# Loops on two engines, aligned loads and a reordered tail in a two-block decode attention kernel

## The chip, the cores and the metric

The kernel runs on one core of one Trainium2 chip. The metric is the device time of one execution in microseconds.

## What is computed

Two independent attention blocks, A and B, decode one token each for a batch of two, with 32 heads of width 192 and a cache of 8192 keys and values per head. Their outputs stand side by side. In block A every head has its own cache too (`rep` is 1), so both blocks do the same work.

```python
def block(x, k_cache, v_cache, wq, wo):          # A and B alike
    B, Sq, D = x.shape                           # 2, 1, 640
    Hq, Dh = 32, 192
    q = (x @ wq).reshape(B, Sq, Hq, Dh).transpose(0, 2, 1, 3)
    scores = jnp.einsum("bhqd,bhkd->bhqk", q, k_cache) * (Dh ** -0.5)
    p = jax.nn.softmax(scores, axis=-1)
    o = jnp.einsum("bhqk,bhkd->bhqd", p, v_cache)
    return o.transpose(0, 2, 1, 3).reshape(B, Sq, Hq * Dh) @ wo
out = concatenate([block(A...), block(B...)], axis=-1)
```

All inputs are bf16. The four caches hold some 805 MB, and each byte of them is used once.

## The kernel before

The work is cut into 64 **units**. A unit is two heads of one batch entry of one block: its K and its V are one load each of 6144 KB, with 64 partitions for each of the two heads and 128 positions of 192 elements (49152 bytes) on every partition. A large tensor `big` in SBUF holds three buffers of that size (`kv`, taken in turn) and two product buffers `prod`, one for a quarter of a unit. Before the loop over units, the query weights lie in `big` as well, and all queries are computed at once into `qall`; at the end the output weights are loaded into buffers that have come free.

For one unit u, in four chunks c of 32 positions:

- VectorE multiplies the chunk of K by the query, `dve_mul`, into `prod[c % 2]` (signal `m, u, c`).
- TensorE sums each position's 192 products to 16 partial sums in PSUM with 12 products by an identity matrix, `pe_sum` (signal `s, u, c`).
- VectorE reduces these 16 to one score, `dve_red` (`r, u, c`); after the last chunk it takes the maximum, `dve_max`.
- GpSimd spreads the maximum over the partitions, `pool_ar`; ScalarE negates it, `act_nb`, and takes the exponentials and their sums, `act_exp`.
- TensorE adds up the sums, `pe_l`, and multiplies the exponentials by V in 64 products, `pe_pv` (`pv, u`). This stands one slot later, after the scores of unit u + 1; for unit 61 it stands two slots later, after the scores of unit 63, next to that of unit 62.
- VectorE takes the reciprocal, and adds the halves (`dve_rc`, `dve_ohi`, `dve_osum`); ScalarE scales the row and puts it back into `qall` (`act_of`).

Each compute engine's instructions are put in a table by slot and order within the slot (`put`), sorted, and added to that engine's `_Stream`. `resolve` turns the named signals into semaphore counts and drops waits that an earlier wait already covers. `emit` writes the instructions; with a `period` it looks (`_find`) for the longest run of slots that repeats every `period` slots with steadily growing counts, writes the part before it in full, then one hardware loop whose waits compare with a register, then the rest in full. In the kernel before, TensorE alone is given `period=6`; VectorE, ScalarE and GpSimd are written out in full.

SyncE issues all large loads in one order: query weights, K 0, then K u and V u - 1 in turn, with K 63 ahead of V 61 near the end, V 62 and V 63, then the output weights in ten pieces. A load waits until its buffer is free: until the last product of the K that it replaces (`m, u, 3`) or the V product (`pv, u`). V 63 is loaded in two halves with signals of their own, both issued after `m, 63, 3`. Block A's output weights wait for `pv, 61` and `s, 63, 3` (they cover V 61's buffer and the product buffers); the first three pieces of block B's wait for `pv, 62`, and the last five for the first half of V 63's product. A matmul `pe_out` for each row of weights then makes the output.

SBUF tensors lie in the order in which they are declared, each rounded up to 32 bytes; the framework puts four small constants of 32 bytes each ahead of the kernel's first tensor. In the kernel before that first tensor is `big`.

Of the kernel before, what the change touches and what calls it, by code (L numbers as in the profile page):

```python
# [5 lines left out]
ALU = mybir.AluOpType  # L6
# [6 lines left out]
class _Stream:  # L13

    def __init__(self, name, sem, reg):
        self.name = name
        self.sem = sem
        self.reg = reg
        self.count = 0
        self.ops = []  # L20

    def add(self, fn, waits=(), sig=None, tag=None):
        if sig is not None:
            self.count += 1
            assert sig not in self.reg, sig
            self.reg[sig] = (self.sem, self.count)
        self.ops.append((fn, tuple(waits), sig is not None, tag))

    def resolve(self):
        waited = {}  # L30
# [14 lines left out]
            out.append((fn, need, has_sig, tag))  # L45
        return out

    def emit(self, eng, period=None):
        ops = self.resolve()
        if period is None:  # L50
            self._emit(eng, ops)
            return
        first, plen, reps, steps = self._find(ops, period)
        self._emit(eng, ops[:first])
        with eng.Fori(0, reps) as it:
            self._emit(eng, ops[first:first + plen], it, steps)
        self._emit(eng, ops[first + plen * reps:])

    def _find(self, ops, period):
# [44 lines left out]
def build_kernel(nc, blocks, out):  # L104
# [5 lines left out]
    TC = 32  # L110
# [21 lines left out]
    with ExitStack() as es:  # L132
        sb = lambda name, shape, dt: es.enter_context(nc.sbuf_tensor(name, shape, dt))
        ps = lambda name, shape, dt: es.enter_context(nc.psum_tensor(name, shape, dt))
        sem = lambda name: es.enter_context(nc.semaphore(name))

        big = sb("big", [128, NBUF * BUFE + 2 * PRODE], BF16)
        qall = sb("qall", [128, NU, Dh], BF16)
        pb = [sb(f"pb{i}", [128, 2 * T], BF16) for i in range(2)]
# [4 lines left out]
        mg = [sb(f"mg{i}", [128, 2], F32) for i in range(2)]  # L144
        nb = [sb(f"nb{i}", [128, 1], F32) for i in range(2)]
        rs = [sb(f"rs{i}", [128, 2], F32) for i in range(2)]
        rc = [sb(f"rc{i}", [2, 1], F32) for i in range(2)]
        ones = sb("ones", [128, 1], F32)
        ident = sb("ident", [128, 128], BF16)
        place = sb("place", [2, 256], BF16)  # L150
        o_hi = sb("o_hi", [2, Dh], F32)
        o_sum = sb("o_sum", [2, Dh], F32)
        oTz = [sb(f"oTz{k}", [128, WR, 6], BF16) for k in range(NBLK)]
        out_sb = [sb(f"out_sb{k}", [4, NH2], BF16) for k in range(NBLK)]
        actd = sb("actd", [128, 2], F32)

        ops = [ps(f"ops{i}", [128, 512], F32) for i in range(2)]
        scps = [ps(f"scps{i}", [128, TC, DG], F32) for i in range(NCH)]
# [63 lines left out]
        def key(name, *idx):  # L222
            for i in idx:
                if i < 0:
                    return None
            return (name,) + tuple(idx)
# [48 lines left out]

        def dve_mul(u, c):
            t = kv[buf["k", u]]
            q = qall[:, u, :].unsqueeze(1).broadcast_to([128, TC, Dh])
            return lambda eng: eng.tensor_tensor(prod[c % 2], t[:, c * TC:(c + 1) * TC, :], q, ALU.mult)  # L279

        def dve_red(u, c):
            return lambda eng: eng.tensor_reduce(sc[u % 2][:, c * TC:(c + 1) * TC], scps[c][:], AXL.X, ALU.add)  # L282
# [1 line left out]
        def dve_max(u):  # L284
            def fn(eng):
                for s in range(2):
                    r = slice(64 * s, 64 * s + 64)
                    ins = eng.tensor_reduce(mp[u % 2][r, s:s + 1], sc[u % 2][r, :], AXL.X, ALU.max)  # L288
                return ins
            return fn  # L290

        def dve_rc(u):
            return lambda eng: eng.reciprocal(rc[u % 2][:], ops[u % 2][0:2, QW:QW + 1])  # L293
# [5 lines left out]
            return lambda eng: eng.tensor_tensor(o_sum[:], ops[u % 2][0:2, 0:Dh], o_hi[:], ALU.add)  # L299

        def act_of(u):
            return lambda eng: eng.activation(qall[0:2, u, :], o_sum[:], ACTF.Identity, scale=rc[u % 2][:])  # L302

        def act_nb(u):
            def fn(eng):
                for s in range(2):
                    r = slice(64 * s, 64 * s + 64)
                    ins = eng.activation(nb[u % 2][r, :], mg[u % 2][r, s:s + 1], ACTF.Identity, scale=-scale)  # L308
                return ins
            return fn  # L310

        def act_exp(u):
            def fn(eng):
                for s in range(2):
                    r = slice(64 * s, 64 * s + 64)
                    dst = pb[u % 2][r, :].rearrange("p (g a j s) -> p g a j s", a=2, j=JB, s=2)[:, :, :, :, s]
                    ins = eng.activation(dst, sc[u % 2][r, :].rearrange("p (g j a) -> p g a j", j=JB, a=2),  # L317
                                         ACTF.Exp, bias=nb[u % 2][r, :], scale=scale, accum_out=rs[u % 2][r, s:s + 1])
                return ins
            return fn  # L320
# [28 lines left out]
        def pe_sum(c):  # L349
            def fn(eng):  # L350
                for j in range(NJ):
                    ins = eng.matmul(scps[c][:], ident[:], prod[c % 2][:, :, j * DG:(j + 1) * DG],  # L352
                                     start=(j == 0), stop=(j == NJ - 1))
                return ins
            return fn

        def pe_l(u):
            return lambda eng: eng.matmul(ops[u % 2][0:2, QW:QW + 1], rs[u % 2][:], ones[:], start=True, stop=True)  # L358

        def pe_pv(u, j0, j1):  # L360
            vv = kv[buf["v", u]].rearrange("p (j a) d -> p j (a d)", a=2)

            def fn(eng):
                for j in range(j0, j1):
                    j0s = 4 * JB * (j // JB) + 2 * (j % JB)
                    ins = eng.matmul(ops[u % 2][0:MP, 0:QW], pb[u % 2][:, j0s:j0s + MP], vv[:, j, :],  # L366
                                     start=(j == 0), stop=(j == TJ - 1))
                return ins
            return fn
# [27 lines left out]
        def put(eng, slot, order, fn, waits, sig, tag=None):  # L397
            t = tabs[eng].setdefault(slot, [])
            t.append((order, len(t), fn, waits, sig, tag))
# [12 lines left out]
        for u in range(NU):  # L412
            for c in range(NCH):
                w = [("k", u), ("qa", u // B), ("qx", u // B), back("s", u, c, 2)]
                if u == 0:
                    w.append(("pq", NP - 1))
                put("dve", u, 2 + 2 * c, dve_mul(u, c), w, ("m", u, c))
                put("dve", u, 2 + 2 * min(c + 1, NCH - 1) + 1, dve_red(u, c),
                    [("s", u, c), key("mx", u - 2), key("exp", u - 2)], ("r", u, c))
                put("pe", u, 0, pe_sum(c),  # L420
                    [("m", u, c), back("r", u, c, NCH), ("id1",), ("qx", NP - 1), ("qa", NP - 1)], ("s", u, c), ("s", c))
            put("dve", u, 12, dve_max(u), [("r", u, NCH - 1), key("ar", u - 2), ("init",)], ("mx", u))
            put("pool", u, 0, pool_ar(u), [("mx", u), key("nb", u - 2)], ("ar", u))
            put("act", u, 0, act_nb(u), [("ar", u), key("exp", u - 2)], ("nb", u))
            put("act", u, 1, act_exp(u), [("nb", u), key("pv", u - 2), key("l", u - 2), ("init",)], ("exp", u))
            w0 = [("exp", u), key("os", u - 2), key("rc", u - 2), ("init",)]
            pslot = u + 2 if u == LASTU - 2 else u + 1
            put("pe", pslot, 2, pe_l(u), w0, ("l", u), ("l", u % 2))
            cuts = VCUT.get(u)
            if cuts is None:  # L430
                put("pe", pslot, 3, pe_pv(u, 0, TJ), [("v", u)], ("pv", u), ("pv", u % 2, buf["v", u]))
            else:
                for c, (t0, t1) in enumerate(zip(cuts[:-1], cuts[1:])):
                    put("pe", pslot, 3 + 0.01 * c, pe_pv(u, t0 // 2, t1 // 2), [("v", u, c)],
                        ("pv", u) if t1 == T else ("pv", u, c))
            put("dve", u + 2, 20, dve_rc(u), [("pv", u), key("of", u - 2)], ("rc", u))
            put("dve", u + 2, 21, dve_ohi(u), [("pv", u), key("os", u - 1)], ("oh", u))
            put("dve", u + 2, 22, dve_osum(u), [("oh", u), key("of", u - 1)], ("os", u))
            put("act", u + 2, 4, act_of(u), [("os", u), ("rc", u)], ("of", u))

        E1, E2 = NU, NU + 1
        for hp in range(NP):
# [25 lines left out]
        for i, (kind, u) in enumerate(loads):  # L468
            w = [done(i - NBUF)]
            if i in (1, 2):  # L470
                w = [("pq", PPB * i - 1)]
            for n, fn in enumerate(ld_kv(kind, u)):
                S_sp.add(fn, waits=w if n == 0 else [])
        for n in range(len(pieces)):
            S_sp.add(ld_wo(n), waits=pieces[n][4])
        S_sp.add(out_dma(NBLK - 1, 1), waits=[("oev", NBLK - 1)])
# [25 lines left out]
        with nc.Block() as block:  # L502
            @block.sync
            def _(eng):
                S_sp.emit(eng)

            @block.gpsimd
            def _(eng):
                S_pool.emit(eng)

            @block.vector
            def _(eng):
                S_dve.emit(eng)

            @block.scalar
            def _(eng):
                S_act.emit(eng)

            @block.tensor
            def _(eng):  # L520
                S_pe.emit(eng, period=6)
# [49 lines left out]
```

## Time and profile before

| | |
|---|---|
| three runs | 1953.11 us median (1952.76 to 1954.46) |
| profiled execution | 1952.38 us |
| its span, first to last instruction | 1950.6 us, 17823 instructions |
| HBM read | 836.77 MB, 429 GB/s over the span |
| granted TensorE clock, mean | 0.943 |

The profile records one execution. A page gives busy times, the span in 40 slices, DMA queues and the chain of work that ended last; further views list instructions in order of time, windows of the span, and the sequencers' instructions by line. [...]

### The profile page before, as it was taken

To read this page: it belongs to the slowest core of one execution; us is meant where nothing else is said; L and a number is where in the kernel's file an instruction comes from. 1 tells how busy PE (TensorE), PEld (TensorE's weight loads), DVE (VectorE), ACT (ScalarE), POOL (GpSimd) and SP (SyncE) were. 2 spreads that over 40 slices of the span, in tenths; PEclk is the share of its full clock that TensorE was granted. 3 is DMA by queue.
4 is the path that set the end of the run, shared out by engine and by line. 5 is a ranking of instruction groups with operands and counts; after the bars stand their busy time and mean duration, and the time that the engine had idled before them with its cause. 6 is when DMAs were issued, how large, how long until landed. Compare 5 with 4: busy or idle time off the path is not lost.

```text
span 1950.6 us, 17823 instructions
## 1 busy us (share of the span) xinstructions
PE 1536.1 (79%) x7781; PEld 747.1 (38%) x7781; DVE 1121.0 (57%) x901; ACT 142.3 (7%) x519; POOL 28.0 (1%) x80
## 2 busy tenths in 40 slices
PE   4787877877877877877777878877888877877889
PEld 2343433433433333433333434433433433333445
DVE  3865565565565565565575565565565565565560
ACT  2100000000000000000000000000000000000000
POOL 0000000000000000000000000000000000000000
PEclk9898999999999999999998988999988999998999
DMA  9999999999999999999999999999999999999998
GB/s 415 433 423 433 433 434 434 432 430 431 433 435 433 434 431 430 433 434 434 434 433 430 432 433 433 434 435 429 433 431 435 433 434 431 432 431 433 433 413 338
DMA packets 20361, 837.20 MB, mean 429 GB/s; under 512 B 2268, under 2 KB 2280, under 8 KB 2920
## 3 DMA queue, kind: packets, MB, share of 16 engines
q1 hardware_dynamic: 20308, 836.77, 99.5%
q8 instruction: 18, 0.29, 0.1%
q14 instruction: 15, 0.12, 0.0%
q10 hardware_dynamic: 20, 0.01, 0.0%
HBM read 836.77 MB, written 0.01 MB: 429 GB/s over the span
## 4 chain that ended last, share of the span: by engine, by line
DMA 47%; PE 32%; DVE 20%; issue 0%; ACT 0%; SPq 0%
DMA big<-in_B_k_cache_dram 24%; DMA big<-in_A_k_cache_dram 21%; PE ops L366 18%; DVE big L279 18%; PE scps L352 12%; DVE sc L282 2%; DMA big<-in_B_wq_dram 2%; PE scps L344 1%; PE outps L388 1%; PE scps L388 1%; PE ops L358 0%; DVE mp L288 0%; PE oTps L375 0%; ACT out_sb L327 0%; DVE qall L269 0%
## 5 line engine op out<-in xcount | busy, mean ns | idle before, releaser
L279 DVE TENSOR_TENSOR big<-big,qall 128x6144 bf16<-128x6144 bf16 x256 | 852.9, 3352 | 512.0 <-DMA big<-in_B_k_cache_dram 258.4
L352 PE MATMUL scps<-big,ident 128*128 128x512 bf16 x3072 | 793.1, 417 | 386.2 <-DVE big L279 386.1
L366 PE MATMUL ops<-big,pb 128*34 128x384 bf16 x4096 | 676.6, 326 | 0.0
L352 PEld LDWEIGHTS scps<-big,ident 128*128 128x128 bf16 x3072 | 307.1, 105 | 864.9 <-DVE big L279 479.8
L366 PEld LDWEIGHTS ops<-big,pb 128*34 128x34 bf16 x4096 | 395.6, 98 | 258.8
L282 DVE TENSOR_REDUCE sc<-scps 128x32 f32<-128x512 f32 x256 | 176.2, 688 | 218.3 <-PE scps L352 218.3
L308 ACT ACTIVATE nb<-mg 64x1 f32<-64x1 f32 x128 | 25.7, 201 | 1703.0 <-POOL mg L260 1702.3
L317 ACT ACTIVATE pb<-sc,nb 64x128 bf16<-64x128 f32 x128 | 55.8, 436 | 11.4 <-PE ops L366 8.5
L260 POOL PARTITION_ALL_REDUCE mg<-mp x64 | 25.8, 404 | 1852.6 <-DVE mp L288 1852.6
L344 PE MATMUL scps<-big,xbc 128*128 128x384 bf16 x160 | 30.8, 361 | 14.2 <-DMA big<-in_A_wq_dram 10.9
L288 DVE TENSOR_REDUCE mp<-sc 64x1 f32<-64x128 f32 x128 | 35.9, 280 | 3.1
L269 DVE CAST qall<-scps 64x192 bf16<-64x192 f32 x64 | 22.7, 354 | 21.3 <-PE scps L344 18.6
L302 ACT ACTIVATE qall<-o_sum,rc 2x192 bf16<-2x192 f32 x64 | 29.0, 453 | 21.8 <-DVE o_sum L299 20.2
L293 DVE RECIPROCAL rc<-ops 2x1 f32<-2x1 f32 x64 | 9.9, 155 | 30.8 <-PE ops L366 28.8
L344 PEld LDWEIGHTS scps<-big,xbc 128*128 128x128 bf16 x160 | 17.0, 107 | 27.7 <-DMA big<-in_A_wq_dram 10.9
L317 ACT ACTIVATION_READ_ACCUMULATOR pb<-sc,nb 64x1 f32 x128 | 23.7, 185 | 0.0
L296 DVE COPY o_hi<-ops 2x192 f32<-2x192 f32 x64 | 22.3, 348 | 2.0
L299 DVE TENSOR_TENSOR o_sum<-ops,o_hi 2x192 f32<-2x192 f32 x64 | 22.1, 345 | 2.2
L273 ACT ACTIVATE qall<-scps 64x192 bf16<-64x192 f32 x64 | 20.8, 325 | 34.5 <-DVE qall L269 32.8
L358 PEld LDWEIGHTS ops<-ones,rs 128*2 128x2 f32 x128 | 5.5, 82 | 26.3 <-issue 26.3
L388 PE MATMUL outps<-big,oTz 128*4 128x320 bf16 x96 | 13.4, 299 | 0.0
L388 PE MATMUL scps<-big,oTz 128*4 128x320 bf16 x96 | 13.2, 299 | 0.0
(27 smaller groups left out, 49.3 us busy)
## 6 DMA issues: line engine op xcount, KB each, us to landing
big<-in_A_k_cache_dram SPq DMA_DIRECT2D x32, 6144.0 KB, 30.0
big<-in_A_v_cache_dram SPq DMA_DIRECT2D x32, 6144.0 KB, 28.1
big<-in_B_k_cache_dram SPq DMA_DIRECT2D x32, 6144.0 KB, 29.0
big<-in_B_v_cache_dram SPq DMA_DIRECT2D x31, 6144.0 KB, 27.9
big<-in_A_wq_dram SPq DMA_DIRECT2D x1, 7680.0 KB, 22.3
big<-in_B_wq_dram SPq DMA_DIRECT2D x1, 7680.0 KB, 39.9
big<-in_B_v_cache_dram SPq DMA_DIRECT2D x2, 3072.0 KB, 18.4
big<-in_A_wo_dram SPq DMA_DIRECT2D x1, 4480.0 KB, 19.3
```

What stands on the lines that cost most here:

```text
L260: return lambda eng: eng.partition_all_reduce(mg[u % 2][:], mp[u % 2][:], 128, bass.bass_isa.ReduceOp.max)
L269: return lambda eng: eng.tensor_copy(qall[ro, B * hp + 1 - s, :], qps[hp % NCH][ri, s * Dh:(s + 1) * Dh])
L279: return lambda eng: eng.tensor_tensor(prod[c % 2], t[:, c * TC:(c + 1) * TC, :], q, ALU.mult)
L282: return lambda eng: eng.tensor_reduce(sc[u % 2][:, c * TC:(c + 1) * TC], scps[c][:], AXL.X, ALU.add)
L288: ins = eng.tensor_reduce(mp[u % 2][r, s:s + 1], sc[u % 2][r, :], AXL.X, ALU.max)
L302: return lambda eng: eng.activation(qall[0:2, u, :], o_sum[:], ACTF.Identity, scale=rc[u % 2][:])
L308: ins = eng.activation(nb[u % 2][r, :], mg[u % 2][r, s:s + 1], ACTF.Identity, scale=-scale)
L317: ins = eng.activation(dst, sc[u % 2][r, :].rearrange("p (g j a) -> p g a j", j=JB, a=2), ACTF.Exp, bias=nb[u % 2][r, :], scale=scale, acc ...
L344: ins = eng.matmul(qps[hp % NCH][:, 0:QW], xbc[:, blk, c, :], wq_t[blk][:, c, off:off + QW], start=(c == 0), stop=(c == DC - 1))
L352: ins = eng.matmul(scps[c][:], ident[:], prod[c % 2][:, :, j * DG:(j + 1) * DG], start=(j == 0), stop=(j == NJ - 1))
L366: ins = eng.matmul(ops[u % 2][0:MP, 0:QW], pb[u % 2][:, j0s:j0s + MP], vv[:, j, :], start=(j == 0), stop=(j == TJ - 1))
L388: ins = eng.matmul(oacc[blk][0:4, 0:NH2], oTz[blk][:, i, 2 - 2 * half:6 - 2 * half], wo[:, i - r0, half * NH2:(half + 1) * NH2], start=(i ...
```

## The change

VectorE and ScalarE get `period=6` as TensorE has it. So that their instructions can stand in a loop, each gets a tag that repeats every six units, and those that address a row of `qall` by the unit take it from a register inside the loop (`row`). Five small tensors are declared ahead of `big`. The chunks 2 and 3 of unit 63's scores get order 4 in TensorE's slot, so that unit 61's row sum and V product (orders 2 and 2.1) stand between chunks 1 and 2; unit 62's get orders 4.5 and 4.6. The halves of V 63 wait apart: the first for `m, 63, 1`, the second for `m, 63, 3`.

```diff
@@ class _Stream
+        self.base = None
...
-        self.ops.append((fn, tuple(waits), sig is not None, tag))
+        self.ops.append((fn, tuple(waits), sig is not None, (-2, object()) if tag is None else tag))
...
+    def row(self, u):
+        return slice(u, u + 1) if self.base is None else bass.ds(self.base + u, 1)
...
         with eng.Fori(0, reps) as it:
+            self.base = it * period
             self._emit(eng, ops[first:first + plen], it, steps)
+        self.base = None
@@ build_kernel
+        actd = sb("actd", [128, 2], F32)
+        rc = [sb(f"rc{i}", [2, 1], F32) for i in range(2)]
+        o_hi = sb("o_hi", [2, Dh], F32)
+        ones = sb("ones", [128, 1], F32)
         big = sb("big", [128, NBUF * BUFE + 2 * PRODE], BF16)
...
-        rc = [sb(f"rc{i}", [2, 1], F32) for i in range(2)]
-        ones = sb("ones", [128, 1], F32)
...
-        o_hi = sb("o_hi", [2, Dh], F32)
...
-        actd = sb("actd", [128, 2], F32)
...
-            q = qall[:, u, :].unsqueeze(1).broadcast_to([128, TC, Dh])
-            return lambda eng: eng.tensor_tensor(prod[c % 2], t[:, c * TC:(c + 1) * TC, :], q, ALU.mult)
+            return lambda eng: eng.tensor_tensor(prod[c % 2], t[:, c * TC:(c + 1) * TC, :],
+                                                 qall[:, S_dve.row(u), :].broadcast_to([128, TC, Dh]), ALU.mult)
...
-            return lambda eng: eng.activation(qall[0:2, u, :], o_sum[:], ACTF.Identity, scale=rc[u % 2][:])
+            return lambda eng: eng.activation(qall[0:2, S_act.row(u), :], o_sum[:].unsqueeze(1), ACTF.Identity, scale=rc[u % 2][:])
...
-                put("dve", u, 2 + 2 * c, dve_mul(u, c), w, ("m", u, c))
+                put("dve", u, 2 + 2 * c, dve_mul(u, c), w, ("m", u, c), ("m", c, u % 6))
...
-                put("pe", u, 0, pe_sum(c),
+                put("pe", u, 4 if u == LASTU and c >= 2 else 0, pe_sum(c),
...
-            put("dve", u, 12, dve_max(u), [("r", u, NCH - 1), key("ar", u - 2), ("init",)], ("mx", u))
+            put("dve", u, 12, dve_max(u), [("r", u, NCH - 1), key("ar", u - 2), ("init",)], ("mx", u), ("mx", u % 6))
...
-            put("pe", pslot, 2, pe_l(u), w0, ("l", u), ("l", u % 2))
+            pe_o = 4.5 if u == LASTU - 1 else 2
+            put("pe", pslot, pe_o, pe_l(u), w0, ("l", u), ("l", u % 2))
...
-                put("pe", pslot, 3, pe_pv(u, 0, TJ), [("v", u)], ("pv", u), ("pv", u % 2, buf["v", u]))
+                put("pe", pslot, pe_o + 0.1, pe_pv(u, 0, TJ), [("v", u)], ("pv", u), ("pv", u % 2, buf["v", u]))
...
             for n, fn in enumerate(ld_kv(kind, u)):
-                S_sp.add(fn, waits=w if n == 0 else [])
+                if (kind, u) == ("v", LASTU):
+                    w = [("m", LASTU, VCUT[u][n + 1] // TC - 1)]
+                S_sp.add(fn, waits=w)
...
-                S_dve.emit(eng)
+                S_dve.emit(eng, period=6)
...
-                S_act.emit(eng)
+                S_act.emit(eng, period=6)
```

The other instructions of VectorE and ScalarE in a slot get tags of the same form (`dve_red`, `act_nb`, `act_exp`, `dve_rc`, `dve_ohi`, `dve_osum`, `act_of`).

More of the change, by code (lines that the diff above doesn't have):

```diff
@@ L416, in build_kernel @@
                     w.append(("pq", NP - 1))
-                put("dve", u, 2 + 2 * c, dve_mul(u, c), w, ("m", u, c))
+                put("dve", u, 2 + 2 * c, dve_mul(u, c), w, ("m", u, c), ("m", c, u % 6))
                 put("dve", u, 2 + 2 * min(c + 1, NCH - 1) + 1, dve_red(u, c),
-                    [("s", u, c), key("mx", u - 2), key("exp", u - 2)], ("r", u, c))
-                put("pe", u, 0, pe_sum(c),
+                    [("s", u, c), key("mx", u - 2), key("exp", u - 2)], ("r", u, c), ("r", c, u % 6))
+                put("pe", u, 4 if u == LASTU and c >= 2 else 0, pe_sum(c),
                     [("m", u, c), back("r", u, c, NCH), ("id1",), ("qx", NP - 1), ("qa", NP - 1)], ("s", u, c), ("s", c))
-            put("dve", u, 12, dve_max(u), [("r", u, NCH - 1), key("ar", u - 2), ("init",)], ("mx", u))
+            put("dve", u, 12, dve_max(u), [("r", u, NCH - 1), key("ar", u - 2), ("init",)], ("mx", u), ("mx", u % 6))
             put("pool", u, 0, pool_ar(u), [("mx", u), key("nb", u - 2)], ("ar", u))
-            put("act", u, 0, act_nb(u), [("ar", u), key("exp", u - 2)], ("nb", u))
-            put("act", u, 1, act_exp(u), [("nb", u), key("pv", u - 2), key("l", u - 2), ("init",)], ("exp", u))
+            put("act", u, 0, act_nb(u), [("ar", u), key("exp", u - 2)], ("nb", u), ("nb", u % 6))
+            put("act", u, 1, act_exp(u), [("nb", u), key("pv", u - 2), key("l", u - 2), ("init",)], ("exp", u), ("exp", u % 6))
             w0 = [("exp", u), key("os", u - 2), key("rc", u - 2), ("init",)]
             pslot = u + 2 if u == LASTU - 2 else u + 1
-            put("pe", pslot, 2, pe_l(u), w0, ("l", u), ("l", u % 2))
+            pe_o = 4.5 if u == LASTU - 1 else 2
+            put("pe", pslot, pe_o, pe_l(u), w0, ("l", u), ("l", u % 2))
             cuts = VCUT.get(u)
             if cuts is None:
-                put("pe", pslot, 3, pe_pv(u, 0, TJ), [("v", u)], ("pv", u), ("pv", u % 2, buf["v", u]))
+                put("pe", pslot, pe_o + 0.1, pe_pv(u, 0, TJ), [("v", u)], ("pv", u), ("pv", u % 2, buf["v", u]))
             else:
@@ L435, in build_kernel @@
                         ("pv", u) if t1 == T else ("pv", u, c))
[L436 to L439, printed above, removed]
+            put("dve", u + 2, 20, dve_rc(u), [("pv", u), key("of", u - 2)], ("rc", u), ("rc", u % 6))
+            put("dve", u + 2, 21, dve_ohi(u), [("pv", u), key("os", u - 1)], ("oh", u), ("oh", u % 6))
+            put("dve", u + 2, 22, dve_osum(u), [("oh", u), key("of", u - 1)], ("os", u), ("os", u % 6))
+            put("act", u + 2, 4, act_of(u), [("os", u), ("rc", u)], ("of", u), ("of", u % 6))
         E1, E2 = NU, NU + 1
```

## The prediction

> **What bounds the kernel now.** I read the page first: engines, slices, DMA queues, the chain's shares, the costliest group.
>
> ```profile
> PE 1536.1 (79%) x7781; PEld 747.1 (38%) x7781; DVE 1121.0 (57%) x901; ACT 142.3 (7%) x519; POOL 28.0 (1%) x80
> ...
> DMA  9999999999999999999999999999999999999998
> GB/s 415 433 423 433 433 434 434 432 430 431 433 435 433 434 431 430 433 434 434 434 433 430 432 433 433 434 435 429 433 431 435 433 434 431 432 431 433 433 413 338
> ...
> q14 instruction: 15, 0.12, 0.0%
> ...
> DMA 47%; PE 32%; DVE 20%; issue 0%; ACT 0%; SPq 0%
> ...
> L279 DVE TENSOR_TENSOR big<-big,qall 128x6144 bf16<-128x6144 bf16 x256 | 852.9, 3352 | 512.0 <-DMA big<-in_B_k_cache_dram 258.4
> ```
>
> The DMA engines are full in every slice but the last, and VectorE idles 512.0 us before its products, waiting for K: 8.0 us in each of 64 units. So only what shortens the stream of loads, or the tail behind it, can count. The chain in order of time clocks the stream, since VectorE's first product of a unit starts when its K has landed.
>
> ```profile
> 275.70 3.37 DVE big L279
> ...
> 1733.88 3.37 DVE big L279
> ...
> 1792.96 3.37 DVE big L279
> ...
> 1822.95 28.13 DMA big<-in_B_k_cache_dram
> 1851.11 6.63 DVE big L279 x2
> ...
> 1862.20 3.28 DVE big L279
> ```
>
> From 1792.96 to 1851.11 four loads of 6144 KB land, 14.54 us each (58.15 / 4). From 1733.88 to 1792.96 four more take 59.08: 0.93 longer. The DMA view of each stretch (the longer first) shows a difference:
>
> ```profile
> q8 instruction: 1, 0.02, 0.1%
> q14 instruction: 1, 0.01, 0.0%
> ```
> ```profile
> q8 instruction: 2, 0.03, 0.2%
> ```
>
> The longer one holds a fetch of instructions on q14, 8 KB each (0.12 MB in 15 packets on the page). The shorter has none, and its two fetches on q8 cost the landing nothing. Between 275.70 and 1851.11 lie 54 units, 108 loads: 1575.41 us against 108 x 14.5375 = 1570.05. The 5.36 us over are 5.8 steps of 0.93, so six.
>
> Whose fetches? VectorE's program is written out in full, and the windows view counts it over that stretch:
>
> ```profile
> 275.70:1851.10 1575.40, 1242.38 (x6157) 597.47 (x6158) 925.22 (x702) 99.94 (x378) 19.15 (x54) 0.94 1.00 433
> ```
>
> Its 702 instructions and two queued waits in each of 54 units (130 in all, a row below) make 810: 135 to each of six fetches, 61 bytes apiece in 8 KB. ScalarE's 378 would need about three. I take the six as VectorE's.
>
> A fetch occupies one DMA engine of 16; that it delays the landing each time means that this engine is the latest already, and falls further behind. The windows view of the tail shows such an engine (the last two columns are DMA share and GB/s), and the DMA view gives the time to landing of V 62, issued when unit 62's last product ends (1862.20 + 3.28 = 1865.5):
>
> ```profile
> 1884.00:1886.00 2.00, 2.00 (x10) 0.68 (x8) 2.00 (x1) 0.00 (x0) 0.00 (x0) 1.00 0.80 344
> 1886.00:1888.00 2.00, 0.90 (x6) 0.42 (x6) 1.66 (x2) 0.00 (x0) 0.00 (x0) 1.00 0.46 197
> 1940.00:1941.00 1.00, 1.00 (x9) 0.61 (x8) 0.00 (x0) 0.00 (x0) 0.00 (x0) 1.00 0.55 205
> ...
> 1942.00:1943.00 1.00, 1.00 (x9) 0.64 (x8) 0.00 (x0) 0.00 (x0) 0.00 (x0) 1.00 0.10 41
> 1943.00:1944.00 1.00, 1.00 (x9) 0.60 (x8) 0.00 (x0) 0.00 (x0) 0.00 (x0) 1.00 0.06 23
> ...
> 1945.00:1946.00 1.00, 1.00 (x9) 0.64 (x8) 0.00 (x0) 0.00 (x0) 0.00 (x0) 1.00 0.03 13
> ```
> ```profile
> big<-in_B_v_cache_dram SPq DMA_DIRECT2D x1, 6144.0 KB, 29.2
> ```
>
> At 1886 to 1888 half of the engines have nothing left (0.46), yet V 62 lands at 1894.7: most engines are some 7 us ahead of the last. At the end a share of 0.06, one engine of 16, works alone from 1943 to about 1945.5.
>
> **The change, part by part.** *Loops on VectorE and ScalarE.* VectorE's 901 instructions and 130 waits (1031) shrink to what is written out (projection and four units, about 124; the last eight units, about 110) and one body of six units. TensorE has such a loop already; its waits cost this:
>
> ```profile
> L96 PEldq ALU_OP  x279: 32/32/42, 132.9 to 1691.4; - x140
> L96 DVEq EVENT_SEMAPHORE  x130: 21/21/49, 57.3 to 1921.9; - x130
> ...
> L55 PEldq COMPARE_BRANCH  x9: 76/208/243, 301.9 to 1701.6; - x9
> ```
>
> Per unit I estimate 13 instructions, two queued waits, ten register operations for waits and twelve for the query's row (three for each of four products): 37, times six is 222. Together about 456, or 3.4 blocks of 135 where there were 7.6. The difference is 4.2, and fetches are whole: 4 or 5 fall away, 3 to 6 with the error of my count. I take 5, since the block in which the loop ends already reaches into the last units: 5 x 0.93 = 4.65 us off every landing of the last units. (ScalarE's body is shorter still; its fetches hit an engine that is not latest, and count nothing.)
>
> The loop's own cost: 22 register operations x 32 ns + 208 ns / 6 = 0.74 us a unit, hidden under VectorE's 8.0 us of waiting for K, and under the queue of loads (the load issued at 1822.95 needs 28.13 us for 14.54 of work). Without that cover it would be 54 x 0.74 = 40 us. A product whose query row is addressed by a register stands nowhere in this trace: between 0 and the 2.0 us that the cover allows each of four products. A gain has no reason here, since the tile and shape stay. I take 0; the sequencer rows, tens of ns, are the nearest.
>
> *Alignment of the loads.* Four constants of 32 bytes lie ahead of `big` in before, so its rows start 128 bytes past a multiple of 256; the change puts 896 bytes more in front (32 + 32 + 32 + 768 + 32), 1024 in all. Every load of this trace starts 128 past such a multiple, so none shows a price; the nearest row is the steady 14.54 us. I take 0, and bound it by rival B on one side and as much loss on the other.
>
> *V product of unit 61 amid unit 63's scores.* TensorE's rows (timeline, then the chain):
>
> ```profile
> 1873.90 8.31 PE L352 MATMUL scps<-big,ident 128*128 128x512 bf16 x24 [3.13 <-DVE big L279]
> 1883.25 2.76 PE L352 MATMUL scps<-big,ident 128*128 128x512 bf16 x12 [1.04 <-DVE big L279]
> 1887.11 2.76 PE L352 MATMUL scps<-big,ident 128*128 128x512 bf16 x12 [1.10 <-DVE big L279]
> ```
> ```profile
> 1889.88 0.17 PE ops L358 x4
> 1890.05 20.91 PE ops L366 x128
> ...
> 1911.34 10.51 PE ops L366 x64
> ...
> 1935.34 13.05 PE scps L388 x96
> 1948.40 0.02 issue
> 1948.42 0.43 ACT out_sb L327
> ```
>
> After the second chunk (1882.2) TensorE waits 1.04 and 1.10 us for VectorE, then never again until 1948.40: the tail is TensorE's. V 61 is there by then (below), so its 64 products (half of 20.91) and their row sums fill these gaps, and chunks 2 and 3 follow without a wait: 2.14 us off TensorE's end. VectorE's products 2 and 3 need only chunks 0 and 1, so the release of K 63 does not move. Unit 63's last chunk ends some 3.7 us later than now (1893.6, worked out below, against 1889.9), and with it its reductions, maximum and exponentials; their first user on TensorE, its V product, stands behind unit 62's 10.5 us. TensorE now waits for V 61 in the middle of the scores; the landing, 1851.1 (issued when K 62 lands) + 29.0 = 1880.1, lies 2.1 us ahead of that place, and both ends move together.
>
> ```profile
> big<-in_B_v_cache_dram SPq DMA_DIRECT2D x1, 6144.0 KB, 29.0
> ```
> ```profile
> 1900.58 0.81 SPq L234 DMA_DIRECT2D big<-in_A_wo_dram  x2
> ```
>
> The first output weights wait for V 61's product and unit 63's scores: now issued when chunk 3 ends, 1887.1 + 2.76 + 10.5 - 2.1 - 4.65 = 1893.6 in place of 1900.58. The queue is then still full of V 63.
>
> *V 63's halves apart.* The first half waits for product 1 of unit 63 instead of product 3, some 10 us earlier. Behind it on SP's queue stand only its other half and the output weights, which wait for later things. It fills the hole of 1884 to 1888, (0.20 + 0.54) x 2 = 1.5 us of the engines that are ahead. The latest engine never ran dry, so this alone moves no end, but it keeps the engines ahead from becoming the next limit.
>
> *Sum.* TensorE's end moves by 4.65 + 2.14 = 6.8. The last output weights are the other limit: the late engine finishes about 1945.5, half a microsecond to land, four products of 13.05 / 96 = 0.14 after that: 1946.6 against 1948.40, 1.8 us to spare. So the end moves by at most 4.65 + 1.8 = 6.45; I take 6.4. The profiled execution took 1952.38 (span 1950.6); it becomes 1946.0. The median of the runs, 1953.11, stands 0.73 above it: 1946.7.
>
> **Rivals.** *B, aligned loads are faster.* 128 bytes more on each row of 49152 (6144 KB over 128 partitions) would be 0.26%, 0.038 us a load, 5.1 us over 837 MB. Then 1946.7 - 5.1 = 1941.6. For it: the rate never passes 435 in the slices; against: nothing shows where the missing part goes. The Trainium skill ("DMA: Bandwidth & Descriptors", How a descriptor splits into AXI transactions) says that a transfer off a 256-byte boundary pays for the bytes below its start, which is this price; no run here shows it. Chance 0.18.
>
> *C, fewer fetches fall away,* three instead of five (a longer body than I count), or another engine takes over as latest at that depth: 2.8 + 1.8 = 4.6, 1948.5. Chance 0.14.
>
> *D, the late engine is late by nature* and the fetches only coincide; the loops then bring nothing, the late engine's weights bind, and 1.8 us are left: 1951.3. Against it: the steps. The Trainium skill ("DMA: Bandwidth & Descriptors", Latency and other measured facts) calls two of the 16 DMA engines usually slower, and puts it down to transfers issued from GpSimd; these are issued from SP. Chance 0.07.
>
> *E, slower: the loop refetches its body.* If VectorE's 222 instructions, 1.6 blocks, are fetched again in each of eight later passes, 16 fetches replace the 5: (16 - 5) x 0.93 = 10.2 us, less 1.8: 1961.5. It decides from about one fetch a pass on. Against it, TensorE's loop body of some 1360 instructions, running from 133 to 1701, shows no q8 fetch between 320 and 1720 (DMA view; q8 would stand between the two lines):
>
> ```profile
> q1 hardware_dynamic: 13865, 606.00, 100.2%
> q14 instruction: 10, 0.08, 0.0%
> ```
>
> Chance 0.07.
>
> **How the numbers follow.** Forecast 0.54 (own range 1945 to 1948), B 0.18, C 0.14, D 0.07, E 0.07. A run of this kernel can tell about 0.2%, 3.9 us. Forecast, B and most of C (0.12) are faster: 0.84; the rest of C and D: 0.09; E: 0.07. The range leaves out D, E and B's far edge: 1941.2 to 1949.6.
>
> **What would show it.** Right: q14 falls from 15 packets to under ten; the chain's VectorE piece at 1851.11 starts near 1846.5; after 276 the loads land 14.54 apart without steps; a V product of 64 stands between two blocks of 24 score matmuls and the weights are issued near 1893.6; the last score-bank matmul ends near 1942. B shows as loads 14.50 apart. Wrong: steps of 0.93 that return every pass, VectorE's wait for K falling under 1 us a unit, or a lone late engine of the same length at the end.

## The result, and the profile after

The changed kernel takes 1941.68 us (median of five runs, 1941.25 to 1942.44) against 1953.05 for the kernel before: 11.4 us less, a ratio of 0.9941 with a 95% interval of 0.9927 to 0.9956. The forecast was 1946.7. The profiled execution took 1941.25, its span 1939.5.

The page, DMA side. Its two queues of the kind "instruction" are q8 and q14. In the runs below only q14's count changes (15, 10 or 7) when VectorE's or ScalarE's program does; q8 stays at 18. As before, the engines are full in every slice but the last; the rate is a little higher, and q14 holds 7 fetches of instructions in place of 15.

```profile
DMA  9999999999999999999999999999999999999998
GB/s 416 433 430 435 434 434 430 434 437 434 431 434 437 434 433 431 438 434 433 431 438 434 433 431 438 433 434 432 437 434 433 432 437 434 433 431 436 432 429 374
...
q14 instruction: 7, 0.06, 0.0%
```

The chain in order of time, start and duration in us. A DMA piece ends when a K has landed.

```profile
1056.82 30.00 DMA big<-in_B_k_cache_dram
...
1114.80 30.01 DMA big<-in_B_k_cache_dram
...
1172.79 30.02 DMA big<-in_B_k_cache_dram
...
1752.68 30.14 DMA big<-in_B_k_cache_dram
...
1810.68 31.10 DMA big<-in_B_k_cache_dram
1841.78 0.02 issue
```

Four loads take 58.00 us (from 1114.80 + 30.01 to 1172.79 + 30.02), 14.50 each, where the kernel before took 14.54. One step is still there: from 1782.82 to 1841.78 it is 58.96. K 62 lands at 1841.78; before, it was 1851.08, 9.3 us later. Five steps of 0.96 that are gone make 4.8, and 123 loads at 0.036 less make 4.4: together 9.2, nearly all of it.

TensorE's tail in the timeline (start, duration, what; idle time and its end in brackets):

```profile
1865.73 7.57 PE L358 MATMUL scps<-big,ident 128*128 128x512 bf16 x24 [3.12 <-DVE big L284]
1873.23 0.19 PE L364 MATMUL ops<-ones,rs 128*2 128x1 f32 x2
1873.35 10.57 PE L372 MATMUL ops<-big,pb 128*34 128x384 bf16 x64
1883.86 5.35 PE L358 MATMUL scps<-big,ident 128*128 128x512 bf16 x24
1889.14 0.19 PE L364 MATMUL ops<-ones,rs 128*2 128x1 f32 x2
```

Unit 61's 64 V products stand between two blocks of 24 score products, and the waits of 1.04 and 1.10 us are gone. TensorE then works without a pause to the last row of the chain below, 1937.28, where it ended at 1948.40 before: 11.1 us, of which 9.3 came with the landings and 1.8 in the tail.

```profile
1924.23 13.05 PE scps L394 x96
1937.28 0.02 issue
```

The 1.8 is a balance of three things. The two waits bring 2.14, and the first 24 score products of unit 63 take 7.57 us in place of 8.31, 0.74 more. But these products start 23.95 us after K 62's landing (1865.73 - 1841.78), where it was 22.82 before: 1.13 lost. The first 12 score products of unit 62, behind that landing, took 2.76 us before and take 4.24 now, and VectorE waits for them. Timeline of before, then chain and window of the changed kernel (the 0.50 is the granted TensorE clock; in the window 1854 to 1858 of before it was 1.00):

```profile
1854.52 2.76 PE L352 MATMUL scps<-big,ident 128*128 128x512 bf16 x12 [0.58 <-DVE big L279]
```
```profile
1845.22 4.24 PE scps L358 x12
```
```profile
1847.00:1849.00 2.00, 2.00 (x6) 0.73 (x5) 1.43 (x1) 0.00 (x0) 0.00 (x0) 0.50 1.02 442
```

Why the granted clock was lower at that place stays open.

The windows view of the end (last two columns DMA share and GB/s) answers to the lone engine of before:

```profile
1930.00:1931.00 1.00, 1.00 (x10) 0.60 (x8) 0.00 (x0) 0.00 (x0) 0.00 (x0) 1.00 1.01 408
...
1934.00:1935.00 1.00, 1.00 (x10) 0.64 (x8) 0.00 (x0) 0.00 (x0) 0.00 (x0) 1.00 0.38 152
1935.00:1936.00 1.00, 1.00 (x9) 0.62 (x8) 0.00 (x0) 0.00 (x0) 0.00 (x0) 1.00 0.19 77
1936.00:1937.00 1.00, 1.00 (x10) 0.52 (x7) 0.00 (x0) 0.00 (x0) 0.00 (x0) 1.00 0.01 5
```

All engines are busy to 1931, and in the microsecond to 1936 the share is 0.19, three engines of 16: they end closer together.

### The profile page after: what moved, and what is told of

It is laid out like the page before. It is cut to its first block, busy times and chain, and to the rows that moved or that the text cites. A ratio compares the mean times of both kernels' runs of the same rounds, so it can differ in the third digit from the quotient of the medians.

```text
span 1939.5 us, 18491 instructions
## 1 busy us (share of the span) xinstructions
PE 1507.2 (78%) x7781; PEld 738.2 (38%) x7781; DVE 1120.2 (58%) x901; ACT 142.3 (7%) x519; POOL 28.0 (1%) x80
## 4 chain that ended last, share of the span: by engine, by line
DMA 48%; PE 28%; DVE 18%; issue 6%; DVEq 0%; ACT 0%; SPq 0%; another core or an unknown queue 0%
DMA big<-in_B_k_cache_dram 25%; DMA big<-in_A_k_cache_dram 21%; PE ops L372 18%; DVE big L284 16%; PE scps L358 7%; DVE sc L288 2%; DMA big<-in_B_wq_dram 2%; PE scps L350 1%; PE outps L394 1%; PE scps L394 1%; PE ops L364 0%; DVEq L284 0%; DVE mp L294 0%; PE oTps L381 0%; ACT out_sb L333 0%
## 5 line engine op out<-in xcount | busy, mean ns | idle before, releaser
L284 DVE TENSOR_TENSOR big<-big,qall 128x6144 bf16<-128x6144 bf16 x256 | 852.9, 3352 | 521.5 <-DMA big<-in_B_k_cache_dram 270.1
L358 PE MATMUL scps<-big,ident 128*128 128x512 bf16 x3072 | 765.1, 405 | 404.4 <-DVE big L284 404.4
L358 PEld LDWEIGHTS scps<-big,ident 128*128 128x128 bf16 x3072 | 298.8, 103 | 863.3 <-DVE big L284 503.3
L308 ACT ACTIVATE qall<-o_sum,rc 2x192 f32 (+1 forms) x64 | 29.0, 453 | 19.9 <-DVE o_sum L305 18.3
```

Of the source, the lines that this page charges most:

```text
L308: return lambda eng: eng.activation(qall[0:2, S_act.row(u), :], o_sum[:].unsqueeze(1), ACTF.Identity, scale=rc[u % 2][:])
```

## Experiments

The forecast left one question: its terms came out, but 5 us more did. Theory T is that three causes add up (five fetches fewer, aligned loads, the tail). The main rival R is that the loops bring the shorter load time too. Each part was run alone first.

### The small tensors ahead of the large one, alone

```diff
 # on the kernel before
+        actd = ...; rc = ...; o_hi = ...; ones = ...      # moved from behind
         big = sb("big", [128, NBUF * BUFE + 2 * PRODE], BF16)
```

> The kernel before with the five small tensors ahead of the large one, nothing else. Theory T (three causes that add up: aligned loads about 0.035 us a load, five fetches fewer at 0.96 us, TensorE's tail about 1.8 us): loads land 14.50 us apart instead of 14.54, the seven steps stay; K 62 lands some 4.4 us earlier than at 1851.1, and the time is 1953.05 - 4.6 = 1948.4. Rival R (the loops alone bring the shorter load time, since the engine sequencers fetch less; alignment is nothing): 1953.0, loads 14.54 apart.

1947.39 us against 1952.82 (ratio 0.9974, 0.9962 to 0.9985). The q14 row is that of before, 15 fetches, and the chain shows K landing 5.0 us earlier at the end (1817.13 + 29.00 = 1846.13):

```profile
1758.50 29.72 DMA big<-in_B_k_cache_dram
...
1817.13 29.00 DMA big<-in_B_k_cache_dram
```

No loop, shorter loads: R is out. The gain of 5.4 is a little over the 4.6 expected. The rows show a reason for part of it: from 1788.22 to 1846.13, right behind a step, it is 57.91, not 58.00. In this kernel about 0.1 us of each step is made up again, which it isn't in the kernel before (58.15 behind the step).

### The loops alone

```diff
 # on the kernel before
-                S_dve.emit(eng)
+                S_dve.emit(eng, period=6)
-                S_act.emit(eng)
+                S_act.emit(eng, period=6)
 # with row() and the tags of the change
```

> The kernel before with loops on VectorE and ScalarE, the tensors and the tail as before. T: loads stay 14.54 apart, two steps instead of seven; K 62 lands 4.8 us earlier; the tail stays bound by TensorE, so 1953.05 - 4.8 = 1948.2. R: loads 14.50 apart, K 62 lands 9.3 us earlier, 1943.7.

1948.46 us against 1952.82 (0.9977, 0.9968 to 0.9986): 4.4 less, near T's 4.8 and far from R's 9.3. K 62 lands at 1816.73 + 29.93 = 1846.66, 4.4 us earlier; q14 falls to 7.

```profile
1816.73 29.93 DMA big<-in_B_k_cache_dram
...
1850.10 5.32 PE scps L359 x12
...
1932.85 13.05 PE scps L395 x96
1945.90 0.02 issue
```

The eleven executions spread over 1947.45 to 1949.87, and the profiled one is the slowest of them: TensorE ends at 1945.90, only 2.5 us earlier than before. The other 1.9 went behind the landing, where the first 12 score products of unit 62 took 5.32 us for 2.76, at a granted clock of 0.50 (window 1850 to 1854). So the end can move by some 2 us with that clock, and only the landings tell the parts apart more finely.

### The tail alone

```diff
 # on the kernel before
-                put("pe", u, 0, pe_sum(c),
+                put("pe", u, 4 if u == LASTU and c >= 2 else 0, pe_sum(c),
 # unit 62's product at 4.5; the halves of V 63 wait apart
```

> The kernel before with the reordered V product and the two halves of the last V waiting apart; no loops, tensors as before. T: landings unchanged; TensorE ends 2.1 us earlier, but the late engine's last weights land at 1946.0 and leave 1.8: 1951.3. A rival (the last weights come earlier too, because half of the last V is issued some 10 us earlier): 1951.0 to 1950.0, with the last landing moved. Nothing at all would be 1953.0.

1950.78 us against 1952.82 (0.9991, 0.9982 to 1.0000): 2.0 less by the medians, though the interval touches 1. The chain shows the limit that the forecast named: TensorE has the gap filled, and at the end waits for the last weights; only four products are left when these land at 1946.2. TensorE ends at 1946.92, 1.5 us earlier than before.

```profile
1893.01 5.29 PE scps L359 x24
...
1933.69 12.50 PE scps L395 x92
1946.19 0.02 issue
1946.20 0.72 PE scps L395 x4
```

The three parts alone make 5.4 + 4.4 + 2.0 = 11.8; together they made 11.4. They add up within the spread of the runs.

### The changed kernel without the alignment

```diff
 # on the changed kernel
-        actd = ...; rc = ...; o_hi = ...; ones = ...      # back behind big
         big = sb("big", [128, NBUF * BUFE + 2 * PRODE], BF16)
```

> The changed kernel with the small tensors back behind the large one: loops and tail stay. T: loads 14.54 apart, two steps, 1941.7 + 4.7 = 1946.4. R: loads 14.50 apart, 1941.7.

1946.18 us against 1952.82 (0.9966, 0.9952 to 0.9979). This is the kernel that the forecast had in effect worked out, 1946.7, since it put the alignment at nothing. K 62 lands at 1846.44 (forecast: near 1846.5), and SP issues the output weights at 1894.51 (forecast 1893.6):

```profile
1817.42 29.02 DMA big<-in_B_k_cache_dram
```
```profile
1894.51 0.80 SPq L241 DMA_DIRECT2D big<-in_A_wo_dram  x2
```

### Which boundary, and does the distance count

```diff
 # on the changed kernel; N = 64, 56 and 8 (256, 224 and 32 bytes)
+        pad = sb("pad", [128, N], F32)
         big = sb("big", [128, NBUF * BUFE + 2 * PRODE], BF16)
```

> The changed kernel with 256 bytes of padding ahead of the large tensor: every load starts 256 bytes past a multiple of 1024. Theory P (a load pays for the bytes between its start and the multiple of 256 below it): nothing changes, loads 14.498 apart, 1941.7. Theory Q (the boundary that counts is 512 or 1024, or the other small tensors' new places matter): back to 14.534 and 1946.3.

> The changed kernel with 224 bytes of padding: loads start 224 bytes past a multiple of 256. P: 224 bytes on each row of 49152 against 128 in the kernel before, so 1.75 times the 0.036 us a load: 14.561 apart, 1941.7 + 8.2 = 1949.9. Rival F (any start off the boundary costs the same): 14.534, 1946.3. Q gives 1946.3 as well.

> The changed kernel with 32 bytes of padding: loads start 32 bytes past a multiple of 256. After the runs at 256 (as fast as the changed kernel) and 224 (loads 14.541 apart, not the 14.561 of theory P), theory F: any start off the multiple of 256 costs about the same, so 14.53 to 14.54 and 1946 to 1947. Theory P would give a quarter of the 128-byte price: 14.509, 1942.9. A third, that only multiples of 32 up to a smaller boundary count and 32 is aligned already: 14.500, 1941.7.

Two K landings from the chain of each, 256, 224 and 32 bytes off, and at last of the kernel without the alignment (128 bytes off); each pair is four loads apart:

```profile
1114.56 30.01 DMA big<-in_B_k_cache_dram
...
1172.55 30.02 DMA big<-in_B_k_cache_dram
```
```profile
1119.98 27.97 DMA big<-in_B_k_cache_dram
...
1178.15 27.96 DMA big<-in_B_k_cache_dram
```
```profile
1119.40 29.02 DMA big<-in_B_k_cache_dram
...
1177.50 29.09 DMA big<-in_B_k_cache_dram
```
```profile
1119.03 28.80 DMA big<-in_B_k_cache_dram
...
1177.17 28.79 DMA big<-in_B_k_cache_dram
```

The column "one row" is the mean time of one packet of 49152 bytes, a row of a load, among all that started between 300 and 1500 us; it is worked out from the times of the DMA packets in each run's trace.

| start past a multiple of 256 | four loads, us | one row, ns | time, us (before, same chip) |
|---|---|---|---|
| 0 (changed kernel, 1024) | 58.00 | 1815.1 | 1941.68 (1953.05) |
| 0 (256 past 1024) | 58.00 | 1815.1 | 1941.64 (1953.36) |
| 32 | 58.17 | 1820.7 | 1947.41 (1952.51) |
| 128 (without the alignment) | 58.13 | 1819.5 | 1946.18 (1952.82) |
| 224 | 58.16 | 1820.7 | 1947.35 (1953.36) |

The boundary is 256 bytes; 1024 is more than is needed, which rules Q out. The price sits in the rows themselves: 4.4 to 5.6 ns on each, and eight of them (128 rows, if 16 engines share them evenly) make the 0.035 to 0.045 us that a load is longer. Padding moves the other tensors behind it too, but it is the loads' own packets that take longer. The distance hardly counts: 32 bytes cost as much as 224. Theory P, a price in proportion to the bytes below the start, was wrong, and F holds. It doesn't hold to the last: 128 bytes cost a fifth less than the other two (0.13 us in four loads against 0.16 and 0.17), and why stays open. The times differ by more, 1.2 us; some 0.9 of it is 123 loads at that difference. At 32 and 224 bytes the chains also end with TensorE waiting for the last weights, as in the tail alone; at 128 the chain doesn't.

### The two halves of the tail

```diff
 # on the changed kernel, one: V product of unit 61 back behind all scores
-                put("pe", u, 4 if u == LASTU and c >= 2 else 0, pe_sum(c),
+                put("pe", u, 0, pe_sum(c),
 # ... and unit 62's row sum and V product at 2 and 3 again, behind unit 61's
 # the other: both halves of V 63 wait for product 3 again
-                    w = [("m", LASTU, VCUT[u][n + 1] // TC - 1)]
-                S_sp.add(fn, waits=w)
+                S_sp.add(fn, waits=w if n == 0 else [])
```

> The changed kernel with unit 61's V product back behind all of unit 63's scores; loops, alignment and the halves' own waits stay. Theory T: TensorE, which waits for nothing else after it, ends its 2.1 us later than in the changed kernel, 1941.7 + 2.1 = 1943.8; landings stay. Rival (the last landing binds anyway): 1941.9.

> The changed kernel with both halves of the last V waiting for the last product of unit 63 again. T: in the changed kernel the engines are less far apart, so the queue does not run dry before the halves are issued: 1941.7, landings unchanged within 0.3. Rival (the earlier half is what moves the last landing): up to 1.5 us later, 1943.2.

Without the order: 1943.59 (0.9952, 0.9938 to 0.9966), 1.9 over the changed kernel, and TensorE's timeline has its waits for VectorE back:

```profile
1875.20 2.76 PE L358 MATMUL scps<-big,ident 128*128 128x512 bf16 x12 [1.46 <-DVE big L284]
1879.06 2.76 PE L358 MATMUL scps<-big,ident 128*128 128x512 bf16 x12 [1.10 <-DVE big L284]
```

Without the halves' own waits: 1941.51, no change. The windows of that run (last two columns DMA share and GB/s) show no hole such as before at 1884 to 1888: with the engines closer together, the queue no longer runs dry there, and the earlier issue has nothing to fill.

```profile
1876.00:1878.00 2.00, 2.00 (x14) 1.18 (x12) 2.00 (x1) 0.00 (x0) 0.00 (x0) 1.00 1.13 492
1878.00:1880.00 2.00, 2.00 (x15) 1.21 (x13) 0.83 (x1) 0.00 (x0) 0.00 (x0) 1.00 1.08 467
```

### Whose fetches count

```diff
 # on the changed kernel, one: ScalarE written out in full
-                S_act.emit(eng, period=6)
+                S_act.emit(eng)
 # the other: VectorE's loop with four passes, 30 units more written out
-                S_dve.emit(eng, period=6)
+                S_dve.emit(eng, period=6, most=4)      # reps = min(reps, most)
```

> The changed kernel with ScalarE written out in full again; VectorE keeps its loop. Theory T (only fetches on the DMA engine that is latest count): ScalarE's four extra fetches, 0.7 us each, fall on an engine 1.7 us ahead of the latest: it overtakes for a while, at most 0.4 us, and the time stays at 1941.7 to 1942.1. Rival (each fetch delays the stream): 4 x 0.96 = 3.8 more, 1945.5.

> The changed kernel with VectorE's loop cut from nine passes to four; the other 30 units are written out, 450 instructions more. T (one fetch for each 8 KB of code, each a step of 0.96 us on the latest engine): five steps in place of two, K 62 lands 2.9 us later, 1941.7 + 2.9 = 1944.6. Rival (the loop as such helps, not the shorter code): the gain shrinks with the passes, 5/9 of 4.8 = 2.7, which is the same time, but without steps, as a longer time between all loads.

ScalarE in full: 1942.04, 0.4 more, which is within the spread of either kernel's runs, with 10 fetches on q14 and no step more in the landings. Its loop is worth next to nothing. VectorE with four passes: 1943.61 (0.9954, 0.9940 to 0.9967). The steps are back where its code is written out:

```profile
1349.51 28.77 DMA big<-in_B_k_cache_dram
...
1407.51 28.77 DMA big<-in_B_k_cache_dram
...
1465.51 29.70 DMA big<-in_B_k_cache_dram
...
1524.03 29.09 DMA big<-in_B_k_cache_dram
```

From 1378.28 to 1436.28 it is 58.00; from 1436.28 to 1495.21 it is 58.93. So the rival (a longer time between all loads) is out. The time rose by 1.9, less than the 2.9 expected. Part of that is that a step doesn't last in full: from 1495.21 to 1553.12, right behind the step, it is 57.91, 0.09 less than 58.00. Over a longer stretch:

```profile
1058.71 28.74 DMA big<-in_B_k_cache_dram
...
1698.01 30.02 DMA big<-in_B_k_cache_dram
```

From 1087.45 to 1728.03, 44 loads, it takes 640.58, where 44 x 14.50 is 638.00: 2.58 for three steps, 0.86 each. Why a step is partly made up where the loads are aligned, and not in the kernel before, stays open.

## Why the prediction was right in direction and too small

The measured gain is 11.4 us where 6.4 was forecast. The mechanism of the terms that were worked out came true; the rest is one term that was put at nothing. The time lies only 0.5 us above the lower edge of the range, and the edge was that low for rival B's sake.

*Fetches.* The step is as forecast: of the six that stand between 275 and 1851 one is left, and five went, 0.96 us each (0.93 in the rows used). (The seventh of which some expectations speak, a fetch at 268.8, stands ahead of that stretch; the changed kernel has one there too.) My count of the program was too high: the changed VectorE program has 362 instructions, not 456 (125 ahead, 138 in the body, 99 behind), because a register serves all four products of a unit, not three operations for each. The difference, 669 instructions over 135, is 4.96 fetches. My count gave 4.2, and that I took 5 from it was in part luck. The loop alone measured 4.4.

*The loop's own cost.* Forecast 0.74 us a unit, hidden. The sequencer rows by line show 432 ALU operations in 54 units, 8 each at 40 ns, and one fused operation for the query row:

```profile
L102 DVEq ALU_OP  x432: 40/40/52, 164.4 to 1716.5; - x144
...
L102 DVEq FUSED_REGOPS  x27: 46/53/53, 158.2 to 1570.2; - x27
...
L284 DVEq FUSED_REGOPS  x54: 57/70/93, 158.0 to 1695.9; - x54
```

That is about 0.42 us a unit without the loop's own end, and no load waits for it. The product addressed by a register takes what it took, as the group's row of the page shows (3352 ns before as well), so the 0 was right.

```profile
L284 DVE TENSOR_TENSOR big<-big,qall 128x6144 bf16<-128x6144 bf16 x256 | 852.9, 3352 | 521.5 <-DMA big<-in_B_k_cache_dram 270.1
```

*Alignment: the term that was mis-sized.* I took 0 because no load of the trace started elsewhere, and gave rival B 0.18. It measured 5.4 alone (4.5 between the changed kernel with and without it). Rival B's time, 1941.6, was right to a tenth, but by luck: by the offsets of 32 and 224 bytes the price is nearly flat for each row, and at 128 bytes B's price in proportion happens to be near it (0.038 us a load against 0.035). The Trainium skill ("DMA: Bandwidth & Descriptors", How a descriptor splits into AXI transactions) has the boundary of 256 bytes that the runs confirm; the beats that its table adds below the start, 1 at 32 bytes and 7 at 224, are not what they show (58.17 at 32 bytes, 58.16 at 224). The page tells it of what is read, and in these runs the start that moved is the one written, in SBUF.

*Tail.* The 2.14 on TensorE came out, and the 1.8 too, but not for the reason given in the changed kernel. There the chain holds no load behind K 62: the 1.8 is 2.14 + 0.74 - 1.13, the last two from the granted clock of two groups of score products, which the forecast didn't look at. That this equals the bound by the last weights is chance. The bound itself is real: the tail alone ran into it. That the halves' own waits move no end was right.

*Rivals C, D and E.* Five fetches went, not three (C). The late engine was late through its fetches (against D). The trace has the 16 moments at which a load's semaphore was raised, which I take as one for each engine. In the kernel before, the last came 0.18 us behind the next at 494 us, 1.18 at 669, 2.1 at 932, 3.1 at 1107, 4.1 at 1282 and 5.4 at 1808, so one engine fell behind with the steps. In the changed kernel it stays at 0.3 to 0.4 from 318 to 1797, and in the windows after, three engines are left where one worked alone. Between 300 and 1700 the changed kernel has no q8 fetch and two on q14, so no loop refetches its body (against E); DMA view:

```profile
q1 hardware_dynamic: 13907, 607.33, 100.2%
q14 instruction: 2, 0.02, 0.0%
```

## What to carry to other kernels

When a kernel is a stream of large loads, look for what the stream carries beside data: here written-out programs were fetched beside it, and a fetch cost something when it fell on the engine that was latest (VectorE's, a step of 0.96 us), and nothing when it did not (ScalarE's). A term for which the trace has no second point ("every load starts 128 bytes off") is not thereby zero; one padded tensor measures it. Where two limits lie 1.8 us apart at the end, an edit of one is worth no more than about that.

## What was not expected of the hardware

A load row that starts off a multiple of 256 bytes in SBUF costs 4.4 ns (128 bytes off) to 5.6 ns (32 or 224) on rows of 49152 bytes that take 1815.1 ns: 0.04 us a load, 5 us of this kernel. Register-addressed VectorE products cost their sequencer 57 to 93 ns once a unit and the engine nothing.
